# A new issue order for a fused chunk-select attention and gated feed-forward kernel

## The chip, the cores and the metric

One core of a Trainium2 chip runs one program. Its engines are TensorE (PE, with its weight loads shown apart as PEld), VectorE (DVE), ScalarE (ACT), GpSimd (POOL) and SyncE (SP, which issues the DMAs here). Each engine takes its instructions in the order in which the program gives them. The metric is device microseconds of one launch, from the median of several runs.

## The reference, cut to what matters

```python
# q, k, v: (4, 8, 768, 64); chunks of 32 keys; top_k = 6
ub = sum_d(max(q * k_min[chunk], q * k_max[chunk]))      # a bound for each query and chunk
ub = where(causal chunk, ub, -1e9)
top_chunks = argsort(ub)[..., -6:]
mask = (key's chunk in top_chunks) & causal
attn = softmax(where(mask, q @ k.T / sqrt(64), -1e9))
x = (attn @ v), heads side by side: (3072, 512)
h = x @ w_in                                             # w_in (512, 2048)
out = (h * clip(h + 3, 0, 6) / 6) @ w_out                # w_out (2048, 512)
```

## The kernel before, in words

The 32 (batch, head) pairs are taken two heads at a time: 16 attention items i, four for each batch. The feed-forward part runs over 8 groups g of 384 tokens, two for each batch (g = 2b holds the low half of the batch's queries, g = 2b + 1 the high half). So groups 0 and 1 need items 0 to 3, groups 2 and 3 items 4 to 7, and so on.

The whole program is one list of 1027 tokens, `ORDER` (line 34), that a loop at line 447 turns into calls. A token such as `S.3.5.a` is: operation S, item 3, unit 5, PSUM tile a. An engine runs its own tokens in the order in which they stand in the list. How far apart two tokens of different engines stand in the list means nothing of itself; semaphores follow from which token writes or reads which buffer first in the list. Two readers of one PSUM tile on different engines go one after the other, in the order of the list.

The operations, by engine:

- PE: `K`, `Q` (L239, six fp32 transposes of a loaded item), `U` (L279, chunk bounds), `T` (L292, transpose of the bounds), `L` (L311, transpose of the selection), `S` (L323 and L331, scores of one of six causal units of an item, and its mask), `A` (L360, values of the low half of the queries), `B` (L360, of the high half, one head each), `X` (L393, transposes of x for groups 0 and 1), `H` (L404, 2 of 16 columns of hidden blocks of a group), `O` (L421, a quarter of the output projection of 128 tokens), `Z` (L231, fourteen matmuls with no use but to start the clock).
- ACT: `kb`, `qb` (L255, L258, bf16 copies), `rp` (L266), `ex` (L337, exponentials of one unit), `hu` (L412, the gate's first half), `ot` (L429, output to SBUF).
- DVE: `mx`, `mn` (L261, chunk maxima and minima), `rn` (L269), `ub` (L284), `t8` (L297, twelve top-8 searches), `sel` (L301), `mt` (L314), `na`, `nb` (L377 and L380, normalisation of the low and high half), `xe` (L397), `gt` (L415, the gate's second half).
- POOL: `vc`, `wc` (L234, L197, casts of values and weights), `af` (L344, causal masks).
- SP: `lk`, `lq`, `lv` (L180, two DMAs each), `wl` (L193, 1 MB of weights), `xt` (L386, three transposing DMAs that bring x into the layout of `H`, for groups 2 to 7), `st` (L433, stores).

PSUM has three wide tiles (a, b, c: for Z, K, Q, U, S, H) and two narrow ones (x, y: for T, L, A, B, X, O). A tile is free for its next writer when the last of its readers is done: after `K` these are `kb`, `mx` and `mn`, after `Q` they are `rp`, `rn` and `qb`, after `H` they are `hu` and then `gt`. SBUF rings also bind: three buffers each for loaded keys, queries and values, two for weights.

The list of before opens like this (four of its 69 lines):

```
PRD PRA lk.0 lq.0 PRP PRL Z.b.14 lk.1 lq.1 K.0.a lv.0 kb.0 mx.0 Q.0.b lv.1 mn.0 rp.0 lk.2 rn.0 qb.0 K.1.c lv.2
U.0.a kb.1 lq.3 Q.1.b ub.0 lk.3 mn.1 T.0.x rp.1 qb.1 t8.0 lq.2 vc.0 lv.3 sel.0 rn.1 L.0.y vc.1 lk.4 mt.0 mx.1
S.0.1.a S.0.3.b ex.0.1 wl.0 S.0.5.c ex.0.3 af.0.1 lq.4 U.1.a ex.0.5 S.0.4.b af.0.3 ub.1 T.1.x af.0.5 ex.0.4
wl.1 S.0.0.a vc.2 t8.1 S.0.2.c lv.4 ex.0.0 K.2.b sel.1 lv.5 ex.0.2 Q.3.a af.0.0 mn.2 L.1.y rp.3 A.0.x af.0.2
```

Of the kernel before, what the change touches and what calls it, by code (L numbers as in the profile page):

```python
# [44 lines left out]
S.2.5.a ex.2.2 af.2.3 lv.8 B.3.1.y af.2.1 S.2.4.c sel.4 ex.2.5 af.2.2 K.5.b nb.3 ex.2.4 af.2.5 S.2.0.a lk.8
mn.5 L.4.x kb.5 B.2.0.y Q.6.c mx.5 ex.2.0 B.2.1.y lq.9 rn.6 rp.6 af.2.0 nb.2 K.6.b qb.6 mt.4 X.1.0.y lk.9 kb.6
mn.6 S.4.1.a S.4.4.c ex.4.1 xe.1.0 A.2.x ex.4.4 af.4.1 Q.5.a mx.6 X.1.1.y lq.8 rp.5 rn.5 U.6.c vc.6 qb.5 na.2
U.5.b ub.6 lv.9 S.4.0.a ub.5 S.4.3.c ex.4.0 xe.1.1 T.5.x H.1.3.b t8.5 ex.4.3 af.4.0 H.1.2.a af.4.3 sel.5
hu.1.3 gt.1.3 wc.2 L.5.y X.0.0.x hu.1.2 S.4.5.c mt.5 xe.0.0 S.5.5.b ex.4.5 A.4.y gt.1.2 X.0.1.x ex.5.5 af.4.5
S.5.1.c wl.4 na.4 S.5.2.a ex.5.1 af.5.5 S.5.3.b xe.0.1 ex.5.2 af.5.1 S.5.4.c T.6.y ex.5.3 H.0.1.a af.5.2 t8.6  # L50
wc.3 ex.5.4 H.0.3.b sel.6 hu.0.1 gt.0.1 H.0.0.c af.5.3 wl.5 hu.0.3 vc.7 gt.0.3 H.1.7.a lv.10 hu.0.0 gt.0.0
H.0.7.b hu.1.7 gt.1.7 B.5.0.x hu.0.7 S.4.2.c H.1.4.a gt.0.7 ex.4.2 af.4.2 S.5.0.b hu.1.4 H.1.0.c ex.5.0 gt.1.4
B.5.1.x af.5.0 hu.1.0 Q.7.b nb.5 A.5.y lq.10 rp.7 gt.1.0 H.1.6.a qb.7 rn.7 vc.9 H.0.4.c hu.1.6 na.5 lv.12
gt.1.6 H.0.2.b hu.0.4 gt.0.4 H.0.5.a wc.4 hu.0.2 gt.0.2 K.7.c hu.0.5 L.6.x B.4.0.y lk.10 mx.7 kb.7 B.4.1.y
# [5 lines left out]
Q.9.c ot.0.1 lv.13 O.1.0.0.y rp.9 rn.9 lq.12 T.7.x qb.9 O.1.0.1.y t8.7 st.0.1 O.1.0.2.y sel.7 O.1.0.3.y L.7.x  # L60
U.9.a ot.1.0 mt.7 st.1.0 S.7.4.b ub.9 S.7.0.c ex.7.4 S.7.1.a T.9.x O.1.1.0.y t8.9 ex.7.0 S.7.3.b ex.7.1 af.7.0
S.7.2.c sel.9 ex.7.3 S.7.5.a af.7.1 L.9.x O.1.1.1.y mt.9 ex.7.2 af.7.3 A.7.x ex.7.5 S.9.1.b af.7.2 na.7
S.9.5.c O.1.1.2.y ex.9.1 af.7.5 xt.2 ex.9.5 af.9.1 B.7.0.x af.9.5 S.9.2.a S.9.3.b ex.9.2 S.9.4.c B.7.1.x
ex.9.3 af.9.2 K.10.a nb.7 vc.11 O.1.1.3.y ex.9.4 lk.13 mn.10 af.9.3 H.2.7.b kb.10 mx.10 lv.14 ot.1.1 H.2.6.c
hu.2.7 xt.3 st.1.1 gt.2.7 H.2.0.a hu.2.6 gt.2.6 T.8.x hu.2.0 H.2.2.b t8.8 O.1.2.0.y hu.2.2 gt.2.0 O.1.2.1.y
sel.8 H.3.2.c gt.2.2 L.8.x O.1.2.2.y hu.3.2 mt.8 S.8.5.a gt.3.2 S.8.4.b ex.8.5 O.1.2.3.y ex.8.4 af.8.5 S.8.1.c
S.8.3.a ex.8.1 S.8.2.b ex.8.3 af.8.1 S.8.0.c B.9.0.x ex.8.2 af.8.3 B.9.1.x H.3.0.a nb.9 ot.1.2 af.8.2 ex.8.0
st.1.2 B.8.0.y B.8.1.y hu.3.0 af.8.0 H.3.4.b nb.8 gt.3.0 A.8.x hu.3.4 H.3.3.c vc.12 na.8 gt.3.4 lv.15 H.3.5.a
hu.3.3 gt.3.3 H.2.1.b hu.3.5 gt.3.5 H.3.7.c hu.2.1 gt.2.1 H.2.3.a hu.3.7 gt.3.7 O.2.2.0.y hu.2.3 H.2.5.b
gt.2.3 O.2.2.1.y hu.2.5 H.2.4.c gt.2.5 K.11.a hu.2.4 Q.10.b lk.14 mx.11 kb.11 O.2.0.0.x rp.10 gt.2.4 lq.13  # L70
O.2.0.1.x qb.10 mn.11 O.2.0.2.x rn.10 O.2.0.3.x U.10.c ot.2.0 S.9.0.a st.2.0 ub.10 O.2.2.2.y ex.9.0 O.2.2.3.y
af.9.0 T.10.x ot.2.2 K.12.b t8.10 st.2.2 A.9.y lk.15 kb.12 Q.11.c vc.13 na.9 Q.12.a rp.11 lq.14 sel.10
O.2.1.0.y qb.11 mn.12 lq.15 L.10.x rp.12 O.2.1.1.y mt.10 qb.12 mx.12 O.2.1.2.y rn.11 S.10.4.b rn.12 U.11.c
ex.10.4 U.12.a ub.11 S.10.0.b ub.12 S.10.3.c ex.10.0 T.12.x O.2.1.3.y t8.12 ex.10.3 af.10.0 S.10.1.a S.10.2.b
ot.2.1 af.10.3 sel.12 S.10.5.c ex.10.1 st.2.1 T.11.y ex.10.2 L.12.x af.10.1 H.3.6.a t8.11 ex.10.5 af.10.2
H.3.1.b sel.11 hu.3.6 af.10.5 mt.12 gt.3.6 L.11.y B.10.0.x hu.3.1 S.12.5.c mt.11 S.11.5.a gt.3.1 ex.12.5
B.10.1.x A.10.y ex.11.5 nb.10 af.12.5 S.11.0.b vc.14 S.11.4.c na.10 ex.11.0 O.3.1.0.x af.11.5 ex.11.4 af.11.0
O.3.1.1.x S.11.1.a S.11.2.b ex.11.1 S.12.4.c ex.11.2 S.12.3.a af.11.1 O.3.0.0.y ex.12.4 af.11.2 O.3.0.1.y
ex.12.3 O.3.0.2.y af.12.3 S.12.1.b S.12.2.c ex.12.1 S.11.3.a ex.12.2 S.12.0.b af.12.1 O.3.0.3.y ex.11.3
# [5 lines left out]
H.4.1.b gt.5.5 H.4.6.c hu.4.1 gt.4.1 H.5.3.a hu.4.6 gt.4.6 T.13.x hu.5.3 H.4.4.b t8.13 H.4.0.c hu.4.4 gt.5.3
sel.13 O.5.1.1.y hu.4.0 gt.4.4 L.13.x H.5.4.a mt.13 gt.4.0 S.13.0.b hu.5.4 S.13.5.c O.4.0.0.x ex.13.0 gt.5.4
O.4.0.1.x ex.13.5 af.13.0 S.13.1.b af.13.5 S.13.2.a ex.13.1 S.13.4.c ex.13.2 S.13.3.b af.13.1 O.4.0.2.x
ex.13.4 af.13.2 O.4.0.3.x ex.13.3 O.5.1.2.y ot.4.0 af.13.3 H.5.6.a st.4.0 B.13.0.x hu.5.6 B.13.1.x Q.15.c
gt.5.6 Q.14.b rp.15 nb.13 O.5.1.3.y qb.15 rn.15 O.4.2.0.x rp.14 rn.14 ot.5.1 O.4.2.1.x qb.14 st.5.1 O.4.2.2.x
O.4.2.3.x A.13.y ot.4.2 U.14.a na.13 st.4.2 U.15.c ub.14 T.14.x ub.15 O.4.1.0.y t8.14 O.4.1.1.y sel.14  # L90
O.4.1.2.y L.14.x O.4.1.3.y mt.14 S.14.4.b ot.4.1 S.14.0.a ex.14.4 st.4.1 S.14.1.c T.15.x O.5.2.0.y t8.15
ex.14.0 S.14.2.b ex.14.1 af.14.0 S.14.5.a sel.15 ex.14.2 S.14.3.c af.14.1 L.15.x O.5.2.1.y mt.15 ex.14.5
af.14.2 A.14.x ex.14.3 af.14.5 S.15.2.b na.14 S.15.1.a S.15.0.c af.14.3 ex.15.2 O.5.2.2.y ex.15.1 af.15.2
B.14.0.x ex.15.0 af.15.1 B.14.1.x O.5.2.3.y nb.14 af.15.0 S.15.3.b ot.5.2 S.15.5.a ex.15.3 st.5.2 S.15.4.c
# [385 lines left out]
```

## Time and profile before

| | |
|---|---|
| runs | 305.55, 307.29, 307.57 us; median 307.29 us |
| profiled execution, first to last instruction | 304.5 us |
| PE busy | 282.3 us (93%) |
| PE weight loads | 176.0 us (58%) |
| ACT, DVE, POOL busy | 181.5, 168.0, 69.8 us |
| mean granted clock of TensorE | 0.994 |
| HBM read, written | 27.26 MB, 6.29 MB |

The page shows the span and no time around it; the median of the runs lies 2.8 us over the span. Busy times of PE are modelled from pipelined matmuls, so a busy PE need not be one that does useful work at its full rate.

### The profile page before, as it was taken

What the parts mean: (1) busy time and instruction counts of PE and PEld (TensorE: products, weight loads), DVE (VectorE), ACT (ScalarE), POOL (GpSimd) and SP (SyncE); (2) the same over time, 40 slices, a digit from 0 to 9 for tenths busy, and PEclk for the clock granted to TensorE, in tenths of its full rate; (3) what the DMA queues carried; (4) which work ended last, traced back from release to release, by engine and by line L of the source; (5) the groups of instructions that cost most, each with busy time, mean ns of one, the idle gap of its engine ahead of it and who ended that gap; (6) DMA issues with size and microseconds to landing.
All of it is one profiled execution on the core that took longest, in us unless ns stands there. A gap on an engine that the chain in (4) does not pass through costs nothing.

```text
span 304.5 us, 7383 instructions
## 1 busy us (share of the span) xinstructions
PE 282.3 (93%) x3036; PEld 176.0 (58%) x3062; DVE 168.0 (55%) x435; ACT 181.5 (60%) x234; POOL 69.8 (23%) x133
## 2 busy tenths in 40 slices
...
PEclk9979999999999999999999999999999999999999
DMA  9999999999589461803058101310001013300111
GB/s 172 218 207 289 256 230 259 247 222 330 124 281 211 115 172 37 174 35 84 5 140 189 39 2 71 69 37 34 2 0 71 37 39 88 88 0 0 69 71 69
DMA packets 92771, 36.40 MB, mean 120 GB/s; under 512 B 85569, under 2 KB 85569, under 8 KB 92737
## 3 DMA queue, kind: packets, MB, share of 16 engines
...
HBM read 27.26 MB, written 6.29 MB: 110 GB/s over the span
## 4 chain that ended last, share of the span: by engine, by line
PE 77%; DVE 9%; ACT 5%; DMA 2%; SPq 2%; issue 2%; DVEq 0%; ACTq 0%
PE PSy L421 14%; PE PSx L421 10%; PE PBa L404 10%; PE PBb L404 9%; PE PBc L404 8%; DVE KM L261 4%; DMA XT<-XB 2%; SPq L386 2%; PE PBb L323 2%; PE PSx L360 2%; PE PSy L360 2%; PE PBc L323 2%; PE PBb L239 2%; ACT KB L255 2%; PE PSx L292 2%
## 5 line engine op out<-in xcount | busy, mean ns | idle before, releaser
L344 POOL TENSOR_SCALAR_AFFINE_SELECT PT<-PT 128x256 bf16<-128x256 bf16 x96 | 38.1, 406 | 155.9 <-ACT PT L337 154.8
L404 PEld LDWEIGHTS <-WIN 128*128 128x128 bf16 x512 | 49.1, 98 | 37.9 <-issue 5.1
L421 PEld LDWEIGHTS <-GT 128*128 128x128 bf16 x384 | 35.8, 98 | 38.2 <-issue 0.9
L421 PE MATMUL PSy<-WOUT,GT 128*128 128x512 bf16 x205 | 51.6, 379 | 1.1 <-issue 0.2
L421 PE MATMUL PSx<-WOUT,GT 128*128 128x512 bf16 x153 | 37.1, 379 | 0.7 <-issue 0.5
L404 PE MATMUL PBa<-XT,WIN 128*128 128x384 bf16 x192 | 35.1, 326 | 1.7 <-DMA XT<-XB 1.6
L337 ACT ACTIVATE PT<-PBb 128x1024 bf16<-128x1024 f32 (+2 forms) x33 | 30.9, 937 | 6.9 <-PE PBb L331 6.4
L415 DVE SCALAR_TENSOR_TENSOR GT<-U,PBa 128x768 bf16<-128x768 bf16 x24 | 22.8, 950 | 21.7 <-ACT U L412 21.5
L404 PE MATMUL PBb<-XT,WIN 128*128 128x384 bf16 x168 | 30.7, 326 | 2.4 <-DMA XT<-XB 2.4
L337 ACT ACTIVATE PT<-PBc 128x1024 bf16<-128x1024 f32 (+2 forms) x33 | 30.7, 932 | 2.3 <-PE PBc L331 2.2
L412 ACT ACTIVATE U<-PBa 128x768 bf16<-128x768 f32 x24 | 19.5, 814 | 20.5 <-PE PBa L404 20.3
L337 ACT ACTIVATE PT<-PBa 128x1024 bf16<-128x1024 f32 (+2 forms) x30 | 26.8, 893 | 6.4 <-PE PBa L331 6.2
L404 PE MATMUL PBc<-XT,WIN 128*128 128x384 bf16 x152 | 27.8, 326 | 0.3 <-DMA XT<-XB 0.3
L360 PEld LDWEIGHTS <-PT 128*128 128x128 bf16 x672 | 24.2, 97 | 4.6 <-issue 1.2
L412 ACT ACTIVATE U<-PBb 128x768 bf16<-128x768 f32 x21 | 17.0, 810 | 16.4 <-PE PBb L404 16.4
L331 PEld LDWEIGHTS <-EM 64*128 64x128 bf16 x448 | 22.6, 95 | 6.1 <-issue 0.5
L415 DVE SCALAR_TENSOR_TENSOR GT<-U,PBb 128x768 bf16<-128x768 bf16 x21 | 20.0, 951 | 10.4 <-ACT U L412 10.3
L412 ACT ACTIVATE U<-PBc 128x768 bf16<-128x768 f32 x19 | 15.4, 812 | 15.0 <-PE PBc L404 15.0
L323 PEld LDWEIGHTS <-KB 64*128 64x128 bf16 x320 | 16.5, 94 | 13.4 <-issue 10.4
L415 DVE SCALAR_TENSOR_TENSOR GT<-U,PBc 128x768 bf16<-128x768 bf16 x19 | 18.1, 952 | 10.5 <-ACT U L412 10.4
L297 DVE MAX8 T<-PSx 96x8 f32<-96x32 f32 x156 | 16.5, 178 | 7.7 <-PE PSx L292 7.6
L234 POOL CAST VB<-VS 128x768 bf16<-128x768 f32 x16 | 13.2, 827 | 27.3 <-PE PSy L360 18.3
...
## 6 DMA issues: line engine op xcount, KB each, us to landing
...
XT<-XB SPq DMA_TRANSPOSE x18, 2.5
```

The source lines that it names most:

```text
L234: nc.gpsimd.tensor_copy(VB[i % 4][:, :, :, 0:D], VS[i % 3][:])
L261: nc.vector.tensor_reduce(out=KM[i % 3][:, m, 0:NCH], in_=cols(slot["K", i], 0, S).rearrange("p (c w) -> p c w", w=CH), axis=AX.X, op=(A.m ...
L297: nc.vector.max(out=T8[i % 2][:, s, :], in_=view[:, s, :])
L323: nc.tensor.matmul(PSB[c][:, e, at:at + n], lhsT=K[rows, j * P:(j + 1) * P], rhs=Q[rows, q0:q0 + n], start=True, stop=q0 + n <= Q0, tile_p ...
L331: nc.tensor.matmul(PSB[c][:, e, at + lo - q0:at + hi - q0], lhsT=EM[rows, j, h, :], rhs=M[rows, lo - Q0 - HQ * h:hi - Q0 - HQ * h], start= ...
L337: nc.scalar.activation(PT[i % 3][u][:, :, 0:n], PSB[slot["S", i, u]][:, :, 0:n], ACT.Exp, scale=float(scale))
L344: nc.gpsimd.affine_select(out=T[:, :, lo:lo + P], in_=T[:, :, lo:lo + P], pattern=[[0, 2], [1, P]], compare_op=A.is_ge, fill=0.0, base=0, ...
L360: nc.tensor.matmul(O[:, e, t, :], lhsT=PT[i % 3][u][:, e, lo:lo + P], rhs=VB[i % 4][:, j, e, :], start=(j == 0), stop=(j == qb))
L404: nc.tensor.matmul(PSB[c][:, ff, 0:GRP], lhsT=WIN[:, kt, (2 * f + ff) * P:(2 * f + ff + 1) * P], rhs=XT[g % 3][:, kt, :], start=(kt == 0), ...
L412: nc.scalar.activation(slot["R", g, f][:], PSB[slot["H", g, f]][:, :, 0:GRP], ACT.Relu, bias=3.0)
L415: nc.vector.scalar_tensor_tensor(out=GT[g % 2][:, 2 * f:2 * f + 2, :], in0=slot["R", g, f][:], scalar=6.0, in1=PSB[slot["H", g, f]][:, :, ...
L421: nc.tensor.matmul(PSS[c][:], lhsT=GT[g % 2][:, f, t * P:(t + 1) * P], rhs=WOUT[:, f, :], start=(f == 0), stop=(f == FT - 1))
```

## The change

Only `ORDER` changes. Both lists hold the same 1027 operations; they differ in the sequence, and in the PSUM tile letters that many PE tokens carry. No instruction is added, removed or altered in shape. The diff replaces all lines of the list; here is its core (the removed lines that the argument uses, then the added ones).

```diff
-wl.1 S.0.0.a vc.2 t8.1 S.0.2.c lv.4 ex.0.0 K.2.b sel.1 lv.5 ex.0.2 Q.3.a af.0.0 mn.2 L.1.y rp.3 A.0.x af.0.2
-lk.5 rn.3 qb.3 K.3.c mt.1 lq.6 mx.2 kb.2 S.1.0.a kb.3 B.0.0.y mx.3 lk.6 S.1.3.b ex.1.0 mn.3 B.0.1.y ex.1.3
-Q.2.a af.1.0 na.0 U.3.c lq.5 rp.2 af.1.3 nb.0 vc.3 S.1.2.b qb.2 ub.3 ex.1.2 rn.2 T.3.x lv.6 S.1.5.c t8.3 U.2.a
...
-B.12.0.x B.12.1.x mn.13 B.11.1.y Q.13.a nb.12 K.15.b rp.13 nb.11 A.12.x qb.13 K.14.c rn.13 xt.5 kb.15 A.11.y
-na.12 U.13.a vc.15 kb.14 na.11 O.3.2.0.x ub.13 xt.4 O.3.2.1.x mn.15 H.5.2.a mx.15 mn.14 H.5.7.b hu.5.2 mx.14
-O.3.2.2.x gt.5.2 hu.5.7 H.4.7.c H.5.0.a hu.4.7 gt.4.7 O.3.2.3.x hu.5.0 H.4.5.c gt.5.0 ot.3.2 st.3.2 gt.5.7
...
-A.15.x O.5.0.0.y ex.15.5 af.15.3 na.15 ex.15.4 af.15.5 O.5.0.1.y xt.6 O.5.0.2.y O.5.0.3.y B.15.0.x ot.5.0
-B.15.1.x st.5.0 H.6.5.b nb.15 xt.7 H.6.7.a hu.6.5 gt.6.5 H.6.0.c hu.6.7 gt.6.7 H.6.2.b hu.6.0 gt.6.0 H.7.5.a
...
-O.7.0.1.y st.7.1 O.7.0.2.y O.7.0.3.y ot.7.0 st.7.0
+PRP PRD Z.b.14 PRA PRL lk.0 K.0.a kb.0 mx.0 lk.2 lq.0 Q.0.b mn.0 rp.0 rn.0 qb.0 K.2.c mn.2 U.0.a ub.0 lq.1 Q.1.b
+T.0.x rp.1 mx.2 lk.1 kb.2 t8.0 K.1.a lq.2 lk.3 Q.2.c qb.1 sel.0 rn.1 L.0.y mt.0 S.0.1.b kb.1 rp.2 ex.0.1 S.0.3.b
+mn.1 mx.1 qb.2 ex.0.3 rn.2 U.1.a lq.4 S.0.0.c af.0.3 ex.0.0 ub.1 S.0.2.b ex.0.2 U.2.a ub.2 S.0.4.c ex.0.4 af.0.1
+lv.2 T.1.x t8.1 lq.3 Q.3.a rp.3 S.0.5.b K.3.c sel.1 ex.0.5 L.1.y T.2.x rn.3 mt.1 S.1.5.b kb.3 mx.3 mn.3 qb.3
+ex.1.5 S.1.0.a ex.1.0 t8.2 sel.2 S.1.2.b ex.1.2 lk.4 S.1.3.c ex.1.3 U.3.a ub.3 S.1.4.b L.2.y mt.2 T.3.x lv.1
+S.2.1.a lv.0 vc.0 ex.1.4 vc.1 ex.2.1 af.0.0 t8.3 sel.3 S.2.3.c af.0.5 ex.2.3 af.1.5 S.1.1.b af.1.0 A.0.y na.0
+ex.1.1 Q.4.a lk.6 S.2.2.c rp.4 rn.4 af.1.2 af.1.3 K.4.b af.0.2 mn.4 af.1.1 L.3.x lq.5 mt.3 ex.2.2 B.1.0.y qb.4
+wl.0 wc.0 kb.4 B.1.1.y S.2.5.c nb.1 ex.2.5 mx.4 S.2.4.a af.2.5 B.0.0.x B.0.1.x nb.0 vc.2 ex.2.4 S.3.3.c S.3.2.b
+ex.3.3 ex.3.2 lv.3 vc.3 af.2.3 U.4.a ub.4 S.3.0.c ex.3.0 af.2.1 A.1.y af.3.2 na.1 T.4.x t8.4 S.3.5.a S.2.0.b
+ex.3.5 S.3.1.c af.2.2 B.2.0.y wl.1 sel.4 ex.3.1 af.3.3 ex.2.0 lk.5 K.5.a S.3.4.c ex.3.4 wc.1 mn.5 L.4.x mt.4
...
+K.7.a mx.7 S.5.4.b A.2.y vc.6 na.2 ex.5.4 H.1.1.c kb.7 mn.7 af.5.5 hu.1.1 gt.1.1 af.4.3 H.1.4.b hu.1.4 sel.6
...
+L.7.y hu.0.3 gt.0.3 O.0.1.0.x lk.11 U.8.b mt.7 S.7.0.a wc.5 hu.0.6 wl.7 gt.0.6 S.7.2.c ub.8 ex.7.0 af.5.0
...
+O.2.2.3.x ot.2.2 na.11 kb.14 lk.15 xt.4 mn.14 mx.14 K.13.a Q.13.b kb.13 mx.13 rp.13 mn.13 qb.13 O.2.0.0.y
...
+na.15 af.15.3 H.5.3.a af.15.2 B.15.0.x B.15.1.x nb.15 hu.5.1 gt.5.1 H.5.4.b hu.5.4 gt.5.4 hu.5.3 A.13.y na.13
+gt.5.3 O.4.0.0.x O.4.0.1.x O.4.0.2.x H.5.7.c H.5.6.b hu.5.7 gt.5.7 hu.5.6 xt.7 gt.5.6 H.5.2.a O.4.0.3.x ot.4.0
+hu.5.2 H.5.5.c hu.5.5 gt.5.2 xt.6 H.6.1.b gt.5.5 hu.6.1 gt.6.1 H.6.0.a hu.6.0 gt.6.0 H.6.3.c H.6.6.b O.5.2.0.y
...
+O.7.1.2.y O.7.1.3.y ot.7.1 O.7.0.1.x st.7.1 O.7.0.2.x O.7.2.0.y O.7.2.1.y O.7.0.3.x ot.7.0 st.7.0 O.7.2.2.y
+O.7.2.3.y ot.7.2 st.7.2
```

## Rows read from the trace of the kernel before

**Rows 1.** Page: busy by engine; busy tenths, granted clock and DMA share in 40 slices
```profile
PE 282.3 (93%) x3036; PEld 176.0 (58%) x3062; DVE 168.0 (55%) x435; ACT 181.5 (60%) x234; POOL 69.8 (23%) x133
...
PEclk9979999999999999999999999999999999999999
DMA  9999999999589461803058101310001013300111
```

**Rows 2.** Window: PE, PEld, DVE, ACT, POOL busy (count), clock, DMA share, GB/s
```profile
60.00:70.00 10.00, 10.00 (x115) 6.82 (x114) 7.92 (x23) 8.11 (x12) 5.86 (x8) 1.00 1.13 227
```

**Rows 3.** Chain that ended last, in order of time: start us, us, what
```profile
45.97 0.82 PE PBb L239 x6
...
55.86 0.65 PE PBb L279 x24
57.88 1.30 PE PBb L404 x8
...
82.09 0.65 PE PBc L239 x6
82.87 0.92 PE PSy L360 x30
...
86.66 1.46 PE PSy L421 x6
...
232.64 3.45 PE PSx L421 x16
...
259.02 1.46 PE PBb L404 x8
...
297.25 3.47 PE PSy L421 x16
```

**Rows 4.** Page, costliest groups: line engine op, count | busy, mean ns | idle before
```profile
L337 ACT ACTIVATE PT<-PBb 128x1024 bf16<-128x1024 f32 (+2 forms) x33 | 30.9, 937 | 6.9 <-PE PBb L331 6.4
...
L415 DVE SCALAR_TENSOR_TENSOR GT<-U,PBb 128x768 bf16<-128x768 bf16 x21 | 20.0, 951 | 10.4 <-ACT U L412 10.3
```

**Rows 5.** Waits, all engines: who waited for whom: us in total, times, longest us
```profile
DVE KM L261 <- ACT KB L255: 19.5, 9, 11.6
...
ACT QB L258 <- DVE RN L269: 5.8, 6, 2.0
...
PE PBb L404 <- DMA XT<-XB: 2.4, 2, 1.7
```

**Rows 6.** Timeline of the opening: start us, us, engine line op, xcount [idle before <-releaser]
```profile
7.64 1.82 DVE L261 TENSOR_REDUCE KM<-PBa 128x24 f32<-128x768 f32 x2 [0.78 <-ACT KB L255]
8.28 0.85 PE L239 MATMUL PBc<-IDENT,KS 128*128 128x128 f32 x6 [0.85 <-DMA KS<-in_k_dram]
...
10.16 0.80 ACT L258 CAST QB<-PBb 128x768 bf16<-128x768 f32 x1 [2.00 <-DVE RN L269]
...
11.89 0.83 POOL L234 CAST VB<-VS 128x768 bf16<-128x768 f32 x1 [6.51 <-DMA VS<-in_v_dram]
...
15.00 0.29 DVE L314 TENSOR_SCALAR MT<-PSy 128x288 bf16<-128x288 bf16 x1
...
30.21 0.54 PE L292 MATMUL PSx<-IDENT,UBX 96*96 96x96 f32 x4 [0.43 <-DVE UBX L284]
```

**Rows 7.** Windows of 2 us: the same columns as the windows above
```profile
12.00:14.00 2.00, 0.22 (x3) 0.02 (x1) 1.97 (x14) 1.26 (x2) 1.03 (x2) 1.00 1.35 218
...
16.00:18.00 2.00, 2.00 (x33) 1.23 (x34) 0.16 (x1) 1.74 (x3) 0.73 (x2) 0.50 1.35 218
```

**Rows 8.** Timeline further on, the same columns as in the opening
```profile
197.24 1.46 PE L404 MATMUL PBa<-XT,WIN 128*128 128x384 bf16 x8 [1.64 <-DMA XT<-XB]
...
251.11 0.34 PE L323 MATMUL PBb<-QB,KB 64*128 64x384 bf16 x2
...
251.56 0.33 PE L323 MATMUL PBa<-QB,KB 64*128 64x384 bf16 x2
...
253.85 3.81 SPq L386 DMA_TRANSPOSE XT<-XB  x3
```

More of the change, by code (lines that the diff above doesn't have):

```diff
@@ L45 @@
[L45 to L54, printed above, removed]
@@ L60 @@
[L60 to L69, printed above, removed]
@@ L70 @@
[L70 to L79, printed above, removed]
@@ L85 @@
[L85 to L94, printed above, removed]
```

68 lines of the change are left out of this document (49 added, 19 removed).

## The prediction

> **What bounds the kernel now.** I began with the page [rows 1]. PE is busy for 93% of the span and every other engine for 60% or less, so at first sight there is little to win. But modelled busy time holds waiting too, so I asked what PE's work takes when nothing holds it up. The chain of waits shows each kind in a place where it runs back to back [rows 3]: an H token 1.30 us, an O token 3.45 / 4 = 0.86, a K or Q 0.655 with little beside it, a U 0.65 to 0.80 (0.69 taken), B 0.92 / 2 = 0.46, and A, 12 matmuls of the same kind, 0.37. The scores of unit 3 of an item take 251.56 - 251.11 = 0.45 [rows 8]; scaled by columns, all six units take 2.13. T is 0.5 [rows 6], and L and X are small (0.2 and 0.35, my estimates by columns). The sum: 64 H 83.2, 96 O 82.8, 32 K and Q 21.0, 16 U 11.0, 16 items of scores 34.2, A and B 20.6, T, L and X 12.6, Z 4.8. That makes 270.2 us, and the last O ends at 300.7 [rows 3]. So PE lost 30.5 us, and 3.8 us follow the last matmul.
>
> To see where it was lost I subtract, at marks in the list, the sum of the PE work that stands ahead from the time at which PE got there. I call this the lag. In before [rows 3, 6]:
>
> - T.3: 18.1 us of work ahead, reached at 30.2, lag 12.1
> - K.5: 30.2 ahead, at 46.0, lag 15.8
> - first H: 38.6 ahead, at 57.9, lag 19.3
> - first O: 66.5 ahead, at 86.7, lag 20.2
> - first H of group 6: 228.7 ahead, at 259.0, lag 30.3
>
> Two thirds of the loss thus lie in the opening, before any feed-forward work can fill PE. From 60 us on PE runs full (10.00 us busy in 60 to 70) while DVE and ACT have room [rows 2]. The opening is bound by turns: readers of a PSUM tile on different engines go one after another. DVE's reductions waited 19.5 us for ACT's K copies, and ACT's Q copies 5.8 us for DVE [rows 5]. A K holds its tile for one copy and two reductions, 0.80 + 1.82 [rows 6], and only three wide tiles exist.
>
> The later 10 us hold one repeated cause: H of a new pair of groups stands right behind the values that it needs, and waits for normalisation, three issues of transposes (3.81 us [rows 8]) and their landing. PE's idle time put down to that is 2.4 us on PBb alone [rows 5], and 1.64 in one wait on PBa [rows 8]. Counted as growth of the lag at the four places it is 1.0 + 2.0 + 0.6 + 1.8 = 5.4 us (an estimate: gap from one token's start to the next, less the first one's price).
>
> **The change part by part.** No work is added or removed, so all sums stay; only waits can move.
>
> *First loads.* Before, loads 3 and 5 of the queue could be used from 8.28 and 11.89 [rows 6], some 1.8 us a load. After, the queue is lk.0, lk.2, lq.0, lq.1, lk.1, lq.2, lk.3, lq.4, lv.2, lq.3: Q.0 is third instead of second, so it comes at 8.3 rather than 6.6. mn.2 and mx.2 now stand in DVE's queue ahead of ub.0 and t8.0, and rn.1 ahead of mt.0. Walking this by hand with the rows' durations: rn.0 ends at 10.5, U.0 at 11.15, ub.0 at 12.0, t8.0 at 14.2, sel.0 at 14.8, rn.1 at 15.55, mt.0 at 15.85. Before, mt.0 ended at 15.29 [rows 6]. This step costs 0.6 us.
>
> *Rest of the opening.* The new list runs the bounds of items 1 and 2 early, keeps item 0's values, their casts and masks for later (POOL has 0.8 us of work ahead of T.3 instead of 7.0), and leaves ACT a queue of exponentials at 0.94 each [rows 4] that no longer waits. My walk by hand goes on: U.1 at 17.9, S.0.0 at 18.7, T.1 at 20.7, K.3 at 22.2, T.3 at 28.5, A.0 at 29.8, B.1.0 at 32.4, A.1 at 37.7, K.5 at 40.5. T.3 has 19.0 us of PE work ahead and K.5 29.3, so the lags are 9.5 and 11.2, against 12.1 and 15.8. The walk has no friction in it (0.05 us for a handover, full clock, loads in time). I give back 1.5 us for that: lag 12.7 at K.5, at about 42.0. The ends are 0 and 4.6, the whole gain.
>
> *From K.5 to the first O.* Here the change does something doubtful. At the new first O, 69.6 us of PE work, 68.5 of DVE and 64.7 of ACT stand ahead; in before at its first O it was 66.5, 63.2 and 59.2. The three engines stay level for longer, so DVE decides, with 68.5 - 29.4 = 39.1 us to do. In before DVE went from T.3 to the first H through 22.1 us of work in 27.7 us, 80%. In my walk from T.3 to K.5 it does 10.2 in 12.0, 85%. With H in the mix (0.95 of DVE for 1.30 of PE [rows 3, 4]) I take 90%, between 80% and 97%: 43.4 us, so the first O comes at 85.4, lag 15.8 against 20.2. At 80% it comes at 90.9 with lag 21.3; at 97% with the walk as it is at 80.8, lag 11.2.
>
> *Transposes.* xt.2 to xt.5 now stand far ahead of the H that needs them: from na.11 to the first H of group 4 there are some 20 us of other work. The tight one is xt.6: na.13 ends after A.13, SP issues xt.7 first, and between A.13 and H.6.1 stand O.4.0, four H and no more, 8.6 us, against some 9 for na.13, the rest of xt.7, three issues and the landing. I charge 0.5 us, and the 5.4 us go.
>
> *The rest.* Before, the other 4.7 us of growth are small gaps between operations of different kinds; these I leave as they are, between 3 and 6. The last H is followed by 13.8 us of O against 12.0, with hu and gt of H.7.3 covered by O.6.2 and O.7.0, so the tail stays at 3.8. SP has new places where a load stands behind a gated one: lv.11 behind st.1.2, lv.15 behind st.3.2, lk.12 behind lk.13. POOL's masks queue behind vc.11 and vc.15, and A.9 then has about as much time as it needs. I charge 0.5, between 0 and 4.
>
> *Sum.* Lag at the end: 15.8 + 4.7 + 0.5 + 0.5 = 21.5 against 30.5, so 9 us less. Against the profiled 304.5 this gives 295.5; the median of the runs is 2.8 above the span, so 298.3. Rounding towards the doubtful side I say 299.
>
> **The clock.** After idle stretches PE's granted clock fell: PE did 0.22 us in 12 to 14, and in 16 to 18 the clock was 0.50 [rows 7], the lower level of 1.2 GHz; the page shows it back by the fourth slice and never low again, though PE still waited until 57 us [rows 1]. My walk has PE as thin from 10 to 18 us, and dense from 18.7. The Trainium skill (TensorE: Matmul & The Clock Gate, "HAM oscillation — how this bites in real kernels") describes a kernel whose waits between short bursts throttle PE again in every round. By that rule the opening would stay low, which is the second rival below; this trace shows one fall only and so speaks rather against it.
>
> **The rivals.**
>
> 1. *The level stretch stalls* (three engines at 80% as before). The first O comes at lag 21.3 and only the transposes help: 21.3 + 5.7 = 27.0 against 30.5, 3.5 us less: 303.8. For it: nothing but the list says that DVE will do better than its 80%. Against it: my walk keeps ACT nearly full from 24 us on. Chance 0.17.
> 2. *The clock stays low in the opening* (slower). From U.0 to K.5 there are 29.3 - 6.8 = 22.5 us of PE work at the full rate; at 1.2 GHz that is 45 us from 9.7 on, so K.5 comes at 54.7 rather than 40.5. That is 14 us more; instead of 1.5 for friction: 295.5 + 12.7 = 308.2, or 311 as a median. It decides once PE stays at half clock for more than 20 us. Against it: rows 7. Chance 0.06.
> 3. *A blocked queue* (slower). wl.0 now is the 16th load and wc.0 stands ahead of the masks of items 2 and 3 on POOL. The DMA share is full for ten slices [rows 1]. If weights land 10 us late, the masks, B.2 and B.3 and all that follow wait, and 10 us take the gain: about 308. By my count 17 loads and two pieces of weights, 8.8 MB, must have landed at K.5; at the 218 to 227 GB/s of [rows 2, 7] that takes 39 to 40 us, so 40.5 is just met. Chance 0.09.
> 4. *The walk holds in full*: lag 11.2 at the first O and 4 more at the end: 15.2, 289.2 in the span, 292 as a median. Chance 0.18.
>
> The forecast itself, a gain of 5 to 12 us (295 to 302), has 0.50.
>
> **How the numbers follow.** Likeliest: 299. Leaving out the slower halves of rivals 2 and 3 and the better half of rival 4, the range is 292 to 306. About 1% (3 us) is what a measurement can tell from no change: below 304.2 counts as faster. Faster: 0.50 + 0.18 + half of rival 1 = 0.76, less a little for causes not thought of: 0.74. Same: the other half of rival 1 and bits of 2 and 3: 0.14. Slower: 0.12.
>
> **What the profile would show.** If right: K.5 at 40 to 43 us with ACT over 90% busy from 25 to 40; the first O at 82 to 88; no wait of PE for XT over 0.6 us; one dip of the clock before 25 us; the last O ending near 292. Wrong if the lag at the first O is 20 or more (rival 1), if the clock is low past 30 us (rival 2), if POOL's casts wait for WS or VS for over 5 us with B behind them (rival 3), or if the lag grows by over 9 us after the first O.

## The result, and the profile after

The new list takes 295.8 us (295.2 to 296.4) where the list of before takes 307.0 beside it: a ratio of 0.9643, 95% interval 0.9614 to 0.9673, or 11.2 us less. The forecast was 299.0, between 292 and 306.

The page of the new kernel (busy time by engine; granted clock and DMA share in 40 slices; the span is 293.5 us):

```profile
PE 278.8 (95%) x3038; PEld 174.7 (60%) x3062; DVE 166.3 (57%) x435; ACT 179.7 (61%) x234; POOL 67.7 (23%) x133
...
PEclk9999999999999999999999999999999999999999
DMA  8999999999771967089603700004301410210031
```

Beside [rows 1], the busy times hardly move, as they must when no work is removed; the span shrinks around them. In this execution the clock has no dip; the mean granted clock of the new list's three other executions is 0.992, 0.998 and 0.993, so the list does not rule one out. The lists differ by one line in length, so an L number of the new kernel is one lower than the same operation's in before.

Windows of both kernels over the opening (us from:to, length, then PE, PEld, DVE, ACT, POOL busy with counts, clock, DMA share, GB/s), first before, then after:

```profile
8.00:20.00 12.00, 8.07 (x105) 4.87 (x107) 7.79 (x24) 6.22 (x9) 3.65 (x6) 0.86 1.35 218
20.00:40.50 20.50, 17.20 (x299) 12.85 (x295) 16.61 (x60) 16.29 (x22) 9.41 (x17) 1.00 1.08 258
40.50:57.00 16.50, 14.18 (x273) 11.07 (x275) 12.07 (x34) 13.03 (x17) 6.09 (x12) 1.00 1.13 263
```

```profile
8.00:20.00 12.00, 9.39 (x145) 6.40 (x147) 10.04 (x26) 8.37 (x12) 0.77 (x2) 1.00 1.35 219
20.00:40.50 20.50, 18.39 (x342) 13.76 (x339) 16.65 (x71) 18.83 (x25) 11.70 (x22) 1.00 1.04 251
40.50:57.00 16.50, 16.25 (x286) 12.40 (x283) 14.60 (x49) 15.69 (x21) 8.47 (x15) 1.00 1.07 271
```

In the same 49 us ACT does 42.9 us of work instead of 35.5, DVE 41.3 instead of 36.5, and PE 145, 342 and 286 matmuls instead of 105, 299 and 273. The DMA engines carry the same stream at about the same rate.

The lag of the prediction (time at which PE reaches a token, less the sum of PE work ahead of it; here by the start of its weight load, with the same prices for all kernels) says where the 11 us lie:

| mark | before | after |
|---|---|---|
| T.3 | reached 30.2, lag 12.1 | 29.0, lag 10.0 |
| K.5 | 45.9, lag 15.7 | 40.6, lag 11.4 |
| first H | 57.6, lag 19.0 | 55.6, lag 13.3 |
| first O | 86.1, lag 19.6 | 84.1, lag 14.6 |
| last O | lag 30.1 | lag 19.1 |

So 5.0 us are won by the first O, and 6.0 after it. Most of the later growth of before at its waits for x is gone; one such wait is left, ahead of group 6. The timeline there (start us, us, engine line op, xcount [idle before <-releaser]):

```profile
226.92 8.67 SPq L385 DMA_TRANSPOSE XT<-XB  x6
...
228.17 2.18 SPq L385 DMA_TRANSPOSE XT<-XB  x1
...
229.31 0.56 DVE L379 TENSOR_TENSOR XB<-PSy,RINV 128x384 bf16<-128x384 f32 x1
...
231.78 3.82 SPq L385 DMA_TRANSPOSE XT<-XB  x3
...
234.89 1.46 PE L403 MATMUL PBc<-XT,WIN 128*128 128x384 bf16 x8
...
237.69 1.46 PE L403 MATMUL PBb<-XT,WIN 128*128 128x384 bf16 x8 [1.33 <-DMA XT<-XB]
...
287.84 1.89 PE L420 MATMUL PSy<-WOUT,GT 128*128 128x512 bf16 x8
...
289.81 0.60 ACT L428 ACTIVATE OT<-PSy 128x512 f32<-128x512 f32 x1 [1.18 <-PE PSy L420]
```

The other two SP rows are parts of the first, from narrower windows: the second issue of xt.7, and the three issues of xt.6. SP is busy with xt.7 when na.13 (the DVE row) ends at 229.87, and starts on xt.6 only at 231.78; H.6.1 waits 1.33 us. The last O ends at 289.7, and 3.8 us follow it, as in before.

### The profile page after: what moved, and what is told of

It reads as the page before. It is cut to its first block, busy times and chain, and to the rows that moved or that the text cites. A ratio compares the mean times of both kernels' runs of the same rounds, so it can differ in the third digit from the quotient of the medians.

```text
span 293.5 us, 7348 instructions
## 1 busy us (share of the span) xinstructions
PE 278.8 (95%) x3038; PEld 174.7 (60%) x3062; DVE 166.3 (57%) x435; ACT 179.7 (61%) x234; POOL 67.7 (23%) x133
## 4 chain that ended last, share of the span: by engine, by line
PE 86%; DVE 5%; DMA 3%; ACT 2%; SPq 1%; issue 1%; ACTq 0%; DVEq 0%
PE PSx L420 15%; PE PSy L420 13%; PE PBb L403 10%; PE PBa L403 9%; PE PBc L403 8%; PE PSy L359 3%; PE PSx L359 3%; PE PBb L322 3%; PE PBc L322 3%; PE PBa L322 2%; PE PBb L238 2%; PE PBc L330 2%; PE PBa L238 2%; PE PBa L278 2%; PE PBb L330 2%; DVE KM L260 2%
## 5 line engine op out<-in xcount | busy, mean ns | idle before, releaser
L343 POOL TENSOR_SCALAR_AFFINE_SELECT PT<-PT 128x256 bf16<-128x256 bf16 x96 | 36.5, 410 | 114.2 <-ACT PT L336 113.9
L420 PE MATMUL PSx<-WOUT,GT 128*128 128x512 bf16 x194 | 47.9, 379 | 0.9 <-issue 0.3
L420 PE MATMUL PSy<-WOUT,GT 128*128 128x512 bf16 x166 | 40.1, 379 | 0.5 <-issue 0.2
L403 PE MATMUL PBb<-XT,WIN 128*128 128x384 bf16 x184 | 33.7, 326 | 1.3 <-DMA XT<-XB 1.3
L414 DVE SCALAR_TENSOR_TENSOR GT<-U,PBb 128x768 bf16<-128x768 bf16 x23 | 21.9, 950 | 19.9 <-ACT U L411 19.9
L411 ACT ACTIVATE U<-PBb 128x768 bf16<-128x768 f32 x23 | 18.7, 811 | 21.1 <-PE PBb L403 21.0
L403 PE MATMUL PBa<-XT,WIN 128*128 128x384 bf16 x168 | 30.7, 326 | 0.1
L403 PE MATMUL PBc<-XT,WIN 128*128 128x384 bf16 x160 | 29.3, 326 | 0.0
L414 DVE SCALAR_TENSOR_TENSOR GT<-U,PBa 128x768 bf16<-128x768 bf16 x21 | 19.9, 948 | 11.4 <-ACT U L411 11.4
L411 ACT ACTIVATE U<-PBa 128x768 bf16<-128x768 f32 x21 | 17.0, 811 | 13.8 <-PE PBa L403 13.8
L414 DVE SCALAR_TENSOR_TENSOR GT<-U,PBc 128x768 bf16<-128x768 bf16 x20 | 19.0, 951 | 10.3 <-PE PSx L420 6.4
L411 ACT ACTIVATE U<-PBc 128x768 bf16<-128x768 f32 x20 | 16.2, 811 | 10.8 <-PE PBc L403 10.8
L233 POOL CAST VB<-VS 128x768 bf16<-128x768 f32 x16 | 13.1, 829 | 27.7 <-DMA VS<-in_v_dram 27.7
L376 DVE RECIPROCAL RINV<-PSx 128x6 f32<-128x6 f32 x13 | 2.5, 192 | 29.2 <-PE PSx L359 29.0
```

Source lines behind the costliest of these rows:

```text
L233: nc.gpsimd.tensor_copy(VB[i % 4][:, :, :, 0:D], VS[i % 3][:])
L343: nc.gpsimd.affine_select(out=T[:, :, lo:lo + P], in_=T[:, :, lo:lo + P], pattern=[[0, 2], [1, P]], compare_op=A.is_ge, fill=0.0, base=0, ...
L403: nc.tensor.matmul(PSB[c][:, ff, 0:GRP], lhsT=WIN[:, kt, (2 * f + ff) * P:(2 * f + ff + 1) * P], rhs=XT[g % 3][:, kt, :], start=(kt == 0), ...
L411: nc.scalar.activation(slot["R", g, f][:], PSB[slot["H", g, f]][:, :, 0:GRP], ACT.Relu, bias=3.0)
L414: nc.vector.scalar_tensor_tensor(out=GT[g % 2][:, 2 * f:2 * f + 2, :], in0=slot["R", g, f][:], scalar=6.0, in1=PSB[slot["H", g, f]][:, :, ...
L420: nc.tensor.matmul(PSS[c][:], lhsT=GT[g % 2][:, f, t * P:(t + 1) * P], rhs=WOUT[:, f, :], start=(f == 0), stop=(f == FT - 1))
```

## The experiments

Theory A, from the prediction: two separate gains, one in the opening (ACT and DVE wait less for turns) and one from the waits for x. Theory B: it is the clock, which dipped in before and not after. Theory C: nearly all of it comes later than the opening.

**Half of each list.** The lists are cut at the first H.

```diff
 e1_old_open_new_rest
-PRP PRD Z.b.14 PRA PRL lk.0 K.0.a ...        (new list up to its first H)
+PRD PRA lk.0 lq.0 PRP PRL Z.b.14 ...         (list of before up to H.1.3.b, then t8.5 ex.4.3 sel.5)
 (all tokens that do not stand above, in the order of the new list)
 e2_new_open_old_rest
 PRP PRD Z.b.14 PRA PRL lk.0 K.0.a ...        (new list up to H.1.1.c, then kb.7 mn.7 sel.6)
-(the rest of the new list)
+(all tokens that do not stand above, in the order of before)
```

> The list of before up to its first H (with the readers of the three PSUM tiles still open), then all other tokens in the new order. Theory A, two places: the new opening is worth 4.3 to 5 us (lag at K.5 15.7 against 11.4, at the first O 19.6 against 14.6) and the rest 6; with the old opening only the rest's 6 us are left, so 301 us, and the lag at the first H of group 0 stays near 19. Theory B, the clock: nearly the whole gain comes from the opening, where the new list keeps the clock at its upper level; then 305 to 307. Theory C, nearly all comes later (transposes and small gaps): 296 to 298.

> The new list up to its first H, then all other tokens in the order of before. Theory A: the opening's 4.3 to 5 us alone, 302 to 303 us, with the three waits for transposes back in the trace. Theory B: 296 to 299. Theory C: 305 to 307.

Measured: e1 303.0 us, ratio to before 0.9903 (0.9865 to 0.9940); e2 304.2 us, 0.9918 (0.9891 to 0.9945). Each lies between A and the theory that gives that half nothing: 3.5 and 2.4 us less than before, together 5.9 of 11.2. The lags tell why. In e1 the opening is that of before (15.4 at K.5); behind the joint the lag rises from 18.9 to 21.4 within 7 us and to 22.3 at the first O, then grows by 4.2 to 26.5, much as the new list does (14.6 to 19.1) and not as before does (19.6 to 30.1). In e2 the first H comes with lag 14.6, then the lag climbs to 17.4 within 10 us and 17.8 at the first O, and the old rest adds its 10.3. So both gains are real, about 6 us for the later part and 4.4 by the first H for the opening, but behind each joint 2 to 3 us are lost. That a half is fitted to the half that it was found with is my reading of this; no run shows which tokens cost it. B and C fall as sole causes.

**The waits for x.**

```diff
 e3_before_free_x, e4_after_free_x
-            nc.sync.dma_start_transpose(XT[g % 3][:, :, t * P:(t + 1) * P], XB[b % 2][:, TPG * half + t, :])
+            nc.sync.dma_start_transpose(XT[2][:, :, t * P:(t + 1) * P], XB[b % 2][:, TPG * half + t, :])
...
-                                 rhs=XT[g % 3][:, kt, :], start=(kt == 0), stop=(kt == KT - 1))
+                                 rhs=XT[g % 2][:, kt, :], start=(kt == 0), stop=(kt == KT - 1))
```

> The list of before, but H of groups 2 to 7 reads the x of group 0 or 1 and the transposing DMAs write a tile that nobody reads: all else is issued as before, and no H waits for a transpose. This leaves the x of six groups out of the result. Theory A: the waits cost before 5.4 us, so 301.6 us. Rival: the time is only handed on to the next wait on PE: 305 to 307.

> The same cut in the new list: H of groups 2 to 7 reads the x of group 0 or 1, and nothing waits for a transpose. Theory A: one wait of 1.3 to 1.7 us ahead of H.6.1 goes, 294.1 us; the rest of the new list has no wait for x to lose. Rival (waits handed on): 295.5 to 296.

Measured: e3 301.3 us, ratio 0.9833 (0.9805 to 0.9860), 5.2 us less than the 306.5 of before beside it; e4 293.6 us, ratio 0.9583 (0.9559 to 0.9607), 2.2 less than the new list's 295.8 (1.8 by the ratios). The lag of e3 ends at 24.9 instead of 30.1 and equals before's until the first of these waits. The 5.4 us of the prediction are confirmed, and they are not handed on. The new list keeps about 2 us of them.

**The clock.**

```diff
 e5_before_filled_gap
-... rn.1 L.0.y vc.1 ...
+... rn.1 Z.a.9 L.0.y vc.1 ...
 e8_after_no_start
-PRP PRD Z.b.14 PRA PRL lk.0 ...
+PRP PRD PRA PRL lk.0 ...
```

> Before, with nine of the matmuls of Z put into the 2.3 us in which PE waits for sel.0 (in front of L.0), on PSUM tile a, which is free there. They take 9 x 0.22 = 1.9 us at the upper clock. If before's dip of the clock (0.72 and 0.50 in 14 to 18 us) cost time, it goes: theory B expects 2 to 4 us less, 303 to 305, and a clock of 1.00 in 14 to 18. Theory A: the opening is held by ACT and DVE, so at most 1 us: 306 to 307.

> The new list without the fourteen matmuls Z that have no use but to start the clock, so that the opening begins at the lower level. Rival 2 of the prediction priced an opening at 1.2 GHz at up to 14 us. If the clock stays low as long as PE has waits: 305 to 309. If it rises as soon as PE is half busy for a while (the new list's PE is 70 to 80% busy from 8 us on): the first K and Q at half rate, 0 to 2 us more, 296 to 298.

Windows of e5 (columns as above):

```profile
12.00:14.00 2.00, 1.88 (x8) 0.67 (x7) 1.97 (x14) 0.98 (x2) 1.03 (x2) 1.00 1.35 218
14.00:16.00 2.00, 1.28 (x19) 0.83 (x21) 1.88 (x4) 0.64 (x2) 0.52 (x1) 1.00 1.35 218
16.00:18.00 2.00, 1.78 (x41) 0.96 (x40) 0.55 (x1) 1.76 (x3) 1.18 (x4) 1.00 1.35 222
```

With the gap filled the dip of [rows 7] is gone, T.3 comes 1.1 us earlier (29.1), and the run takes 306.0 us, ratio 0.9968 (0.9943 to 0.9993): 0.7 us less by the medians, 0.2 to 1.7 by the interval, where theory B expected 2 to 4. So theory B is worth at most a sixth of the gain. e8 is the reverse: 296.9 us, ratio 0.9673 (0.9646 to 0.9699), 1.1 us more than the new list by the medians, though the intervals overlap. Four of its K and Q (timeline) and its windows from 18 us on:

```profile
4.68 1.51 PE L238 MATMUL PBa<-IDENT,KS 128*128 128x128 f32 x6 [4.68 <-DMA KS<-in_k_dram]
...
8.28 1.51 PE L238 MATMUL PBb<-IDENT,QS 128*128 128x128 f32 x6 [2.09 <-DMA QS<-in_q_dram]
9.59 1.49 PE L238 MATMUL PBc<-IDENT,KS 128*128 128x128 f32 x6
...
13.20 0.82 PE L238 MATMUL PBa<-IDENT,KS 128*128 128x128 f32 x6
...
18.00:20.00 2.00, 1.94 (x34) 1.10 (x36) 1.25 (x3) 0.95 (x1) 0.77 (x2) 0.59 1.35 218
20.00:22.00 2.00, 2.00 (x38) 1.10 (x32) 0.00 (x0) 1.80 (x2) 0.00 (x0) 0.55 1.35 222
22.00:24.00 2.00, 2.00 (x36) 1.46 (x26) 1.32 (x9) 1.22 (x3) 0.00 (x0) 1.00 0.86 150
```

The first three take 1.5 us, against 0.82 later in this run and after Z in the new list, and a dip follows at 18 to 22 us, yet T.3 comes only 1.1 us later and K.5 0.9: PE has waits in this stretch, and at 1.2 GHz it is still nearly quick enough.

The opening of e7 (below) is the new list's, token for token, and its trace does have a dip (windows of e7):

```profile
16.00:18.00 2.00, 1.19 (x14) 0.71 (x13) 2.00 (x5) 1.81 (x3) 0.00 (x0) 0.87 1.32 221
18.00:20.00 2.00, 2.00 (x32) 0.89 (x30) 1.00 (x3) 1.02 (x1) 0.69 (x2) 0.50 1.33 222
20.00:22.00 2.00, 2.00 (x44) 1.28 (x42) 0.27 (x1) 1.52 (x2) 0.08 (x1) 0.78 1.07 185
```

There the first K starts 1.1 us later than in the new list's trace (6.82 against 5.72), T.1 2.1 later, T.3 0.9 and the first O 0.6. So a late start and a dip together cost little by the first O, and single traces of one opening differ by such amounts.

**The first loads, and the order of transposes.**

```diff
 e6_after_lq0_second
-... mx.0 lk.2 lq.0 Q.0.b ...
+... mx.0 lq.0 lk.2 Q.0.b ...
 e7_after_xt6_first
-hu.5.7 gt.5.7 hu.5.6 xt.7 gt.5.6 ... gt.5.2 xt.6 H.6.1.b
+hu.5.7 gt.5.7 hu.5.6 xt.6 xt.7 gt.5.6 ... gt.5.2 H.6.1.b
```

> The new list with lq.0 ahead of lk.2, as the second load. Q.0 comes 1.6 us earlier (6.7 instead of 8.3). If the first step of the opening sets it, 0.5 to 1.5 us less (294.3 to 295.3); if DVE's queue, full from 10 to 18 us, sets it, less than 0.3 us.

> The new list with the three transposes of group 6 issued ahead of those of group 7. SP then issues them at 229.9, when na.13 ends, instead of after three of group 7; H.6.1 waits 1.3 us there now. Expected 1.0 to 1.5 us less (294.3 to 294.8); if transposes are slower to land side by side with others than issue suggests, no change.

e6: 295.3 us, ratio 0.9626 (0.9599 to 0.9653), 0.5 us less by the medians and not to be told from the new list's 0.9643. Q.0 does come at 6.7, 1.6 us earlier, but T.1 only 0.2 earlier (20.1 against 20.4): up to there DVE's queue is the limit (7.92 us busy of 8 in 10 to 18 in the new list). Behind T.1 another load is. Q.3 waits for its own, in the new list (first two rows of PE's waits; the first is Q.0's) and for 1.4 us in e6, where that load lands no earlier (21.9 us, 21.7 in the new list; the profile puts this wait down to DVE's t8.1, which Q.3 does not depend on). T.3 is reached at 29.1 as in the new list (29.0).

```profile
PE PBb L238 <- DMA QS<-in_q_dram: 1.6, 1, 1.6
...
PE PBa L238 <- DMA QS<-in_q_dram: 1.0, 1, 1.0
```

e7: 294.8 us, 0.9628 (0.9583 to 0.9674); the interval does not separate it either, but its trace shows the wait gone. Timeline of e7:

```profile
230.55 7.86 SPq L385 DMA_TRANSPOSE XT<-XB  x6
...
235.51 1.46 PE L403 MATMUL PBc<-XT,WIN 128*128 128x384 bf16 x8
236.81 1.46 PE L403 MATMUL PBb<-XT,WIN 128*128 128x384 bf16 x8
```

H.6.1 follows H.5.5 without a wait, and the lag stays at 18.3 across that place where the new list's goes from 17.6 to 19.3. So the residue was SP's order: xt.7 issued ahead of xt.6.

**The turns.** Here I expected the mechanism of my prediction to show itself. Both lists have the same order of readers for each of the 16 items. Waits of ACT and DVE for one another in 8 to 57 us (who, for whom: us, times, longest), before, then after:

```profile
ACT QB L258 <- DVE RN L269: 4.5, 4, 2.0
...
ACT KB L255 <- DVE KM L261: 2.3, 3, 1.1
...
DVE KM L261 <- ACT KB L255: 5.7, 6, 1.6
```

```profile
ACT QB L257 <- DVE RN L268: 0.8, 1, 0.8
...
DVE RN L268 <- ACT RP L265: 1.5, 3, 0.7
DVE KM L260 <- ACT KB L254: 1.2, 2, 0.8
```

Counted alike, 13.1 us of such waits became 3.5: for before, 0.6 us in which rn waits for rp are added to the rows shown. In both, some waits of rp for DVE are left out (0.8 us before, 1.3 after). The next two kernels keep each engine's own sequence, token for token, and change only which of two readers on different engines goes first.

```diff
 e9_before_one_turn, e10_after_one_turn (13 exchanges each)
-rp.i ... rn.i ... qb.i        (items 0, 3, 4, 5, 9, 14)
+rp.i ... qb.i ... rn.i
-mn.i ... kb.i ... mx.i        (items 4, 5, 7 to 11; 7, 9 and 11 with mx first)
+kb.i ... mn.i ... mx.i
```

> The list of before with every engine's own sequence kept, token for token; only the order between ACT and DVE among the readers of one PSUM tile is changed, so that each tile is handed over once: rp, qb, rn instead of rp, rn, qb (items 0, 3, 4, 5, 9, 14), and kb ahead of both reductions where it stood between them (items 4, 5, 7 to 11). Theory A (turns hold the opening back): of the 12.5 us that ACT and DVE wait for each other in 8 to 57 us, ACT's 4.5 us for DVE go, and the lag at K.5 falls by 1 to 3 us: 304 to 306. Rival: what matters is what stands ready in the queue, not the number of turns; DVE then waits for ACT instead, and the time stays or grows: 306.5 to 308.

> The same in the new list, which has the same order of readers for each of the 16 items as before. ACT waits for DVE only 0.8 us for qb here, so there is little to win: theory A expects no change within 1 us (295 to 296.5); a loss of over 1 us would show that the new list relies on rn coming early (U needs it).

Measured: e9 310.1 us, ratio 1.0107 (1.0088 to 1.0125); e10 305.1 us, 0.9936 (0.9913 to 0.9959), 9.3 us more than the new list. My expectation for e9 was wrong, and e10's loss is far over anything I named. In e9 ACT no longer waits for rn, but DVE waits 8.6 us for ACT's copies instead of 5.7; the lag at K.5 falls by 0.5 us only, and the later items lose: 20.4 at the first O, 34.0 at the end. In e10 the whole gain of the opening is lost: lag 13.1 at T.3, 15.5 at K.5, 23.6 at the first O, 4.0 more than in before; the rest grows by 5.6, little more than in the new list (4.5). Its timeline around rn.3, and behind it the waits of DVE up to 67 us:

```profile
24.90 0.83 ACT L257 CAST QB<-PBa 128x768 bf16<-128x768 f32 x1
25.76 0.76 DVE L268 TENSOR_SCALAR RN<-PBa 128x576 f32<-128x576 f32 x1 [2.48 <-ACT QB L257]
26.44 0.30 DVE L313 TENSOR_SCALAR MT<-PSy 128x288 bf16<-128x288 bf16 x1
...
26.79 0.34 PE L330 MATMUL PBb<-MT,EM 64*128 64x96 bf16 x4 [1.92 <-DVE MT L313]
27.17 0.81 ACT L336 ACTIVATE PT<-PBb 128x768 bf16<-128x768 f32 x1 [1.44 <-PE PBb L330]
...
DVE RN L268 <- ACT QB L257: 6.9, 4, 2.5
DVE KM L260 <- ACT KB L254: 4.6, 3, 2.3
```

In the new list rn.3 starts at 23.49 and mt.1 at 24.16. In e10 DVE stands idle for 2.48 us before rn.3, which waits for ACT's copies, mt.1 stands behind rn.3 on DVE, the scores of item 1 behind mt.1 on PE, and ACT's exponentials behind those. The clock does not explain e10: its trace has a fall (0.52 in 28 to 30 us), but an execution at a mean clock of 1.000 took 304.1 us. So it is not the number of turns that counts but what stands behind the engine that waits.

**One exchange alone, and a mended list.**

```diff
 e12_after_one_pair
-... L.1.y T.2.x rn.3 mt.1 S.1.5.b kb.3 mx.3 mn.3 qb.3 ex.1.5 ...
+... L.1.y T.2.x kb.3 qb.3 rn.3 mt.1 S.1.5.b mx.3 mn.3 ex.1.5 ...
 e11_after_mended (new list with)
-lk.2 lq.0 ... lq.4 ... lv.2 ... lq.3 ... xt.7 ... xt.6
+lq.0 lk.2 ... lq.3 lq.4 ... lv.2 ... xt.6 xt.7
```

> The new list with a single pair of readers exchanged between engines: qb.3 ahead of rn.3 instead of behind it. Each engine's own sequence stays token for token. With 13 such pairs exchanged the list took 305.1 us, and rn.3 waited 2.5 us for qb.3 there, with mt.1 and so every score of item 1 behind it on DVE. Theory A (the order of readers across engines is itself part of the schedule): 1.5 to 3 us more, 297.3 to 298.8, all of it between T.1 and T.3. Rival (only the sum of many pairs matters, the list has slack for one): within 0.7 us of 295.8.

> The new list with three DMA tokens moved: lq.0 ahead of lk.2, lq.3 ahead of lq.4 and lv.2 (Q.3 waits 1.0 us for its load in the new list and 1.4 with lq.0 moved alone), and xt.6 ahead of xt.7. Alone, lq.0 gave 0.5 us and xt.6 1.0 us. If they add up and Q.3's wait was on the path (rp.3, rn.3, mt.1, kb.3 behind it), 1.5 to 2.5 us under the new list's 295.8: 293.3 to 294.3. If DVE and ACT set the opening whatever the loads do, 1.0 to 1.5 us: 294.3 to 294.8.

e12: 296.7 us, ratio 0.9650 (0.9627 to 0.9672): 1.0 us more by the medians, 0.2 by the ratios, and by the intervals not to be told from the new list. So in time the run does not bear theory A's 1.5 to 3 us out. Its trace shows the loss and how most of it is made up. T.3 is reached at 32.1, 3.1 us later than in the new list; but 1.7 us of that are there at T.1, ahead of the exchanged pair, with a first K 1.0 us late and a dip of the clock (0.50 in 18 to 20 us). Beside e7, which starts as late and dips there too, T.1 is 0.4 us earlier and T.3 2.2 later. At the first O the lag is 16.7, against 15.2 in e7 and 14.6 in the new list. Windows of e12:

```profile
24.00:26.00 2.00, 1.40 (x14) 0.81 (x13) 0.50 (x1) 2.00 (x3) 0.00 (x0) 1.00 0.95 180
26.00:28.00 2.00, 0.85 (x10) 0.64 (x11) 1.87 (x4) 0.40 (x2) 1.62 (x3) 0.78 1.07 236
28.00:30.00 2.00, 1.79 (x22) 1.18 (x20) 2.00 (x13) 1.79 (x3) 1.93 (x6) 0.50 1.06 218
```

DVE stands idle (1.62 us of it before rn.3, for qb.3), then ACT, PE does little, and the clock dips a second time. The mechanism is shown for one pair; its price in the whole run is uncertain, and the profiled execution is the slowest of the four (297.2 us, mean clock 0.988; the others 296.1 to 296.9 at 1.000).

e11: 294.5 us, ratio 0.9576 (0.9551 to 0.9602), the fastest of the kernels that leave nothing out: 1.3 us under the new list by the medians, and with an interval of the ratio that lies below the new list's. In its trace Q.3's load lands at 17.4 instead of 21.7 and T.3 comes at 27.5, 1.5 us earlier than in the new list. So that load was a limit of the new list's opening. But K.5 comes at 41.3, 0.6 later, because PE now waits there for a load (waits of PE, whole run):

```profile
PE PBa L238 <- DMA QS<-in_q_dram: 1.4, 1, 1.4
PE PBa L238 <- DMA KS<-in_k_dram: 1.4, 1, 1.4
```

The KS wait is at K.5. e2, whose opening is the new list's, waits 1.4 us for keys on that tile too, with K.5 reached at 42.0. The same loads are queued ahead of lk.5 in all of them, and lk.5 lands at 40.3 in the new list, 41.2 in e11 and 41.9 in e2: the new list's K.5, at 40.6, stands just behind the load stream, and an opening that is faster ahead of it gains nothing more at this mark.

Where e11's gain comes from its trace does not show. The profiled execution took 295.4 us, one of the two slowest of its six and no faster than the new list's (295.2): its lag is 16.2 at the first O, 1.7 more than the new list's, and 19.3 at the end. It does show that xt.6's wait is gone: the lag no longer grows at H.6.1 (19.3 on both sides).

## Why the prediction was right, point by point

- **Bounds and the sum of PE work.** Right in that the loss on PE is what fell: the lag at the end from 30.1 to 19.1, while the tail stayed at 3.8 us. The sum itself is rough. The scores' 2.13 us an item follow the columns of the masks; by all columns of scores and masks the same 0.45 us give 2.25, 1.8 us more in the sum. It is the same in both lists, so the difference of the lags at the end does not move.
- **First loads.** Q.0 came at 8.34, where the walk had 8.3. Its price of 0.6 us was half of that: mt.0 ended at 15.53, against 15.29 in before, and e6, which gives the load back, has it 0.3 us earlier. By T.3 nothing of it is left, because Q.3 waits for its load in between.
- **The opening.** The walk by hand said 28.5 for T.3 and 40.5 for K.5; the trace has 29.0 and 40.6. The 1.5 us that I gave back for friction were not needed, in part by luck. The loads were not all in time: Q.3 waited 1.0 us for its load, and K.3 came at 23.1 instead of 22.2, but earlier marks had come up to 0.6 us ahead of the walk (U.1 at 17.3 for 17.9). K.5's load landed 0.3 us before K.5. And this execution had no dip of the clock, of which I had expected one. This is one of the two mis-sized terms (lag at K.5 11.4, not 12.7).
- **Why the opening is quicker.** Half right. The waits of ACT and DVE for each other did shrink, from 13.1 to 3.5 us. But the 19.5 us that I quoted for DVE are those of the whole run, with one wait of 11.6 [rows 5]; 5.7 of them lie in 8 to 57 us. And I spoke of turns as a toll on each tile, while e9 shows that fewer turns are no gain. My reading is that the new list changes what is ready in each engine's queue when its turn comes; e10 and the trace of e12 show how closely that depends on who goes first, but no run isolates it as the source of the opening's gain.
- **From K.5 to the first O.** Right in the number, by luck: the stretch took 84.1 - 40.6 = 43.5 us, where I had 43.4, but the profile does not show DVE deciding it. DVE was busy for 36.7 us of it (84%, not 90), ACT for 35.3, while PE's own work there, 69.6 - 29.3 = 40.3 us by the prices, is 93% of the stretch. Ahead of it ACT was as full as I had said: 14.59 us of 15 in 25 to 40.
- **Transposes.** The 5.4 us were there (e3: 5.2). The residue was sized too small: 0.5 said, 1.33 us of wait and 1.7 of lag measured, and 1.8 to 2.2 by e4; so the sign of being right that named no wait over 0.6 us failed. The step that was mis-sized is the path of some 9 us from A.13 to the landing. xt.6's own issues took 3.82 us, as three of before did (3.81 [rows 8]). But one issue of xt.7 ahead of them took 2.18 us, where the other two took 1.2 to 1.3, and the last transpose landed 1.95 us after its issue was done, where that of before took 1.23.
- **The rest.** The other mis-sized term. I kept 4.7 + 0.5 us of small losses after the first O; the new list has 4.5 - 1.7 = 2.8. Which gaps went no run isolates. Load tokens behind gated ones did not hurt: after 57 us the only wait of PE for a DMA in its list of waits is the one for XT.
- **The rivals.** The clock: no dip in the profiled execution, one in e7's, and e8's opening, at the lower level for some 10 us, cost 1 us. My price of 14 us was for 45 us at that level with PE setting the pace throughout. The Trainium skill (TensorE: Matmul & The Clock Gate, "HAM oscillation — how this bites in real kernels") describes a kernel that is throttled again in each round of short bursts and waits. The traces agree in part: e12 falls twice (0.50 in 18 to 20 us and again in 28 to 30), but before, e7 and e10 fall once, e8 once after its low start, and none falls again behind the opening while PE works. Level stretch: the lag at the first O was 14.6, far from 21.3. A blocked queue: PE waits for no blocked load in the new list beyond Q.3's 1.0 us, but K.5 stands 0.3 us behind its load, and e11 and e2 wait there.

Against the forecast of 299 the result is 3.2 us lower. In the span it is 2.0 (295.5 said, 293.5 measured): 1.2 by the first O (lag 14.6 for 15.8), 2.4 less lost in the rest, 1.2 more at the transposes, and 0.4 for the start of the count, since the lag of before is 30.1 by weight loads and 30.5 by matmuls. The median lies 2.3 over the span instead of 2.8, and 0.7 was my rounding to the doubtful side. The 2.8 is no constant: every execution with both figures has the time 1.7 us over its span (295.2 and 293.5), and the rest is how far the profiled execution lies under the median.
